# Bucketed attention with a gated convolution layer: value product in two-step groups, rows divided after the product, rounding casts on another engine

## The chip, the cores and the metric

The kernel runs on one core of one Trainium2 chip. A core has engines that work side by side, each through its own list of instructions in order: PE (TensorE, matrix products; its weight loads are shown apart as PEld), DVE (VectorE), ACT (ScalarE), POOL (GpSimd), and SP, which here only issues DMAs. PE writes only to PSUM, a small memory beside it; POOL in this kernel works on SBUF alone. The metric is the device time of one execution in microseconds (us); the figure of a kernel is the median of its timed runs.

## The reference

There are 4 batches of 8 heads, 768 positions and head size 64. A query and a key may meet only if six sign bits of their projections agree.

```python
mask = q_bucket[:, :, :, None] == k_bucket[:, :, None, :]
scores = scale * np.matmul(q, k.transpose(0, 1, 3, 2))
scores = np.where(mask, scores, -1000000000.0)
scores = scores - np.max(scores, axis=-1, keepdims=True)
attn = np.exp(scores)
attn = attn / (np.sum(attn, axis=-1, keepdims=True) + 1e-09)
attn_out = np.matmul(attn, v)                  # then [B, S, H*D] as x
# gate_pre: causal convolution of x over 5 positions, weights conv_w per channel
gate = 1.0 / (1.0 + np.exp(-gate_pre))
out = (gate * (x @ w_val)) @ w_out
```

All is in float32. The second layer (512 by 512 matrices) is computed with three products each, of numbers split into a rounded part and a rest (the kernel calls the rounded type FP32R).

## The kernel before

**Units, tiles, slots.** A unit is one head of one batch (32 units). A tile is 128 queries of a unit against its 768 keys (6 tiles per unit, 192 in all). The main loop (L453) takes one turn, here called a slot, for each tile; everything else is cut into steps that are handed out to the slots. The order of the instructions on PE, ACT, DVE and POOL is the program's own order (`manual_schedule`, L442); SP's order is left to the compiler.

**One slot k** does, in program order: `keep_transposed(k-4)` on ACT (L289, two copies from PSUM to the tiles `pt`); `maxima(k)` (L238), `factors(k)` (L244) and `shifts(k)` (L248) on DVE, which give the bias `nb` and the scale `gs` of the exponential; for every second tile the sums of two tiles plus a small number and their reciprocals on DVE (L262, L266); `normalise(k-2)` on POOL (L271), which divides the 128x768 tile of exponentials `p` in place; `scores(k+1)` on PE (L232, four products into the PSUM tile `s`); `exponentials(k)` on ACT (L256, with the row sum as a by-product); a step of the convolution (every second slot before slot 60), of the loading of weights (L90 to L112, until about slot 50), of the second layer (`moe`, PE L365 and L390), of the operands of a later unit (`prep`, L166 to L176, six DMAs among them), and one step of the value product; last `transposes(k-3)` on PE (L280, six transposes into two PSUM tiles `tp`).

**Buffers that bind.** There are two PSUM tiles `s`, so `scores(k+2)` cannot start before `exponentials(k)` has read its tile, two tiles `tp`, and one PSUM tile `av` for the value product.

**The value product** `attn_v` (L294) is a generator of six steps, one for each block of 128 keys. A step is two products, for the two halves of the queries, placed in the two column halves of the array (`tile_position`); each appears as two instructions, so the profile shows x4 per step. After the sixth step ACT copies the two halves of `av` into rows of `x`, two heads on top of each other (L311). When a pair of heads is there, `pair_x` splits `x` into a rounded part `xh` (DVE, L323) and the rest `xl` (POOL, L324), and computes the convolution on DVE (L332 once, L334 four times); after four pairs ACT applies the sigmoid (L338) and the second layer of that batch begins. There `ht` (L370, DVE) multiplies by the gate, `hh` (L374, DVE) rounds and `hl` (L376, POOL) is the rest.

The second layer gives work to PE in most slots: a step of its first product (L365) or of its second (L390); a batch has 24 and 18 such steps in 48 slots, six of them taken three to a slot, so that about ten slots of each batch have none.

Of the kernel before, what the change touches and what calls it, by code (L numbers as in the profile page):

```python
# [8 lines left out]
FP32 = mybir.dt.float32  # L9
# [12 lines left out]
# the high word of the float64 2**-127, read as a float32; smaller weights count as zero  # L22
# [4 lines left out]
def kernel(  # L27
    ctx: ExitStack,
    tc: tile.TileContext,
    qk: bass.AP,      # [B, H, 128, S]   rows 0-63: q^T, rows 64-127: k^T  # L30
    v: bass.AP,       # [B, H/2, 128, S/128, 128]
    proj: bass.AP,    # [128, 68]  projection, its signs, and what makes the mask's rows of bits
    w_val: bass.AP,   # [128, 4, 512]
    conv_w: bass.AP,  # [128, 20]
    w_out: bass.AP,   # [128, 4, 512]
    out: bass.AP,     # [B, S, 512]
):
    nc = tc.nc
# [7 lines left out]
    LAG = 3  # L46
# [16 lines left out]
    op = ctx.enter_context(tc.tile_pool(name="op", bufs=2))  # L63

# [19 lines left out]
    # Work beside the scores is cut into steps, at most one of a kind in a slot.  # L84

    def from_float64(w, t):
        """Float64 words w, in place: their high words become float32 numbers, their low words what is left."""
# [69 lines left out]
    def prep(i):  # L157
        """The operands of a unit's scores, each [128, S]: two products add up to them."""
# [7 lines left out]
        nc.vector.tensor_copy(out=aq, in_=r)  # L166
# [19 lines left out]
    def bits(i):  # L186
        """The sign bits of four units' queries and keys, each with its complement."""
# [17 lines left out]
    def first_prep():  # L205
        """The first unit's operands, straight from its own queries and keys."""
# [34 lines left out]
    def factors(k):  # L241
        """The scale of a row, or 0 where it has no key in its query's bucket: all its keys count alike then."""
        gs[k] = small.tile([P, 1], FP32, name="gs")
        nc.vector.tensor_scalar(out=gs[k], in0=nms[k], scalar1=BIG / 2, scalar2=scale, op0=ALU.is_lt, op1=ALU.mult)  # L244

    def shifts(k):
        nbs[k] = small.tile([P, 1], FP32, name="nb")
        nc.vector.tensor_tensor(out=nbs[k], in0=nms.pop(k), in1=gs[k], op=ALU.mult)  # L248

    def exponentials(k):  # L250
        s, nb = ss.pop(k), nbs.pop(k)
        p = pp.tile([P, 2, HS], FP32, name="p")
        if k % 2 == 0:
            cur["sm"] = small.tile([P, 2], FP32, name="sm")
        sm = cur["sm"]
        nc.scalar.activation(out=p, in_=s[:, :, 0:HS], func=AF.Exp, bias=nb, scale=gs.pop(k), accum_out=sm[:, k % 2:k % 2 + 1])  # L256
        ps[k] = (p.rearrange("p a b -> p (a b)"), sm)

    # two tiles' sums at a time
    def row_sums(k):  # L260
        sums[k] = small.tile([P, 2], FP32, name="s1")
        nc.vector.tensor_scalar(out=sums[k], in0=ps[k][1], scalar1=1e-9, scalar2=None, op0=ALU.add)  # L262

    def recip(k):
        ri = small.tile([P, 2], FP32, name="ri")
        nc.vector.reciprocal(out=ri, in_=sums.pop(k))  # L266
        rcs[k], rcs[k + 1] = ri[:, 0:1], ri[:, 1:2]

    def normalise(k):
        p, _ = ps[k]  # L270
        nc.gpsimd.tensor_scalar(out=p, in0=p, scalar1=rcs.pop(k), scalar2=1.0, op0=ALU.mult, op1=ALU.mult)  # L271

    def transposes(k):
        p, _ = ps.pop(k)
# [19 lines left out]
    def attn_v(i, pts):  # L294
# [13 lines left out]
        x = cur["x"]  # L308
        for s in range(2):
            o = KW - 1 + s * HS  # L310
            nc.scalar.copy(out=x[hh * D:(hh + 1) * D, o:o + HS], in_=av[s * D:(s + 1) * D, 0:HS])  # L311
# [5 lines left out]
    def pair_x(b, c, x, gs, xs_):  # L317
        for o in (0, HS):
# [4 lines left out]
            nc.vector.tensor_copy(out=xh, in_=x0)  # L323
# [4 lines left out]
        for k in range(KW):  # L328
            yield
            w = cw_sb[:, c * KW + k:c * KW + k + 1]  # L330
            if k == 0:
                nc.vector.tensor_scalar(out=g, in0=x[:, 0:S], scalar1=w, scalar2=None, op0=ALU.mult)  # L332
# [17 lines left out]
    def moe(b, xs_, g):  # L350
# [7 lines left out]
        def val(o, j):  # L358
# [13 lines left out]
            def split():  # L372
                hh = hp.tile([P, HS], FP32R, name="hh")
                nc.vector.tensor_copy(out=hh, in_=ht)  # L374
# [45 lines left out]
    # units of attention: one head of one batch  # L420
# [134 lines left out]
```

## Time and profile before

| what | value |
|---|---|
| time, three runs | median 647.04 us, 646.44 to 647.19 |
| profiled execution | span 645.6 us from the first to the last instruction; the page gives no other time of it |
| instructions | 10637 |
| busy | PE 610.7 us, PEld 412.7, DVE 489.4, ACT 424.5, POOL 355.5 |
| granted TensorE clock | 0.991 on the mean |
| DMA | 56.76 MB, nearly all on SP's queue |

A busy PE is not PE at its peak. Rows of groups show: line, engine, operation, written tile <- read tiles, shape, count, then busy time and mean time of one, then idle time of the engine in front of them. Rows of a timeline show the start, the duration, and the same names. Slots are told apart below by their place in a unit: the product of unit i takes slots 6i+9 to 6i+14.

### The profile page before, as it was taken

The numbers are of one execution on the slowest core, as the hardware profiler recorded it, in microseconds if no ns is written. First come the engines' busy times: TensorE is split into PE (matmuls) and PEld (weight loads), VectorE is DVE, ScalarE is ACT, GpSimd is POOL, SyncE is SP. The second block draws the span as 40 slices with busy tenths as digits, with TensorE's granted clock in tenths as the row PEclk, the third lists the DMA queues.
The fourth block names the chain that finished last, engine by engine and source line by source line (L and its number), as shares of the span: only waits on it lengthen the run. The fifth ranks groups of instructions, "written<-read, shape, count | busy, mean of one in ns | idle before, by whom it ended". The sixth has DMA issues, their size and how long they took to land.

```text
span 645.6 us, 10637 instructions
## 1 busy us (share of the span) xinstructions
PE 610.7 (95%) x3496; PEld 412.7 (64%) x3496; DVE 489.4 (76%) x1064; ACT 424.5 (66%) x881; POOL 355.5 (55%) x326
## 2 busy tenths in 40 slices
PE   4799998988999999999999999999999999999997
PEld 2565554555557666676667776676657777666895
DVE  5788999999996876769785887658695787656532
ACT  3487776767778666667878676576788666665300
POOL 1375868577765663566653656456563566536221
PEclk9799999999999999999999999999999999999999
DMA  6533435343432324233333234243332313300111
GB/s 239 126 100 78 137 102 136 110 123 89 104 78 66 81 66 133 70 103 95 103 79 104 59 79 118 71 117 79 99 75 60 79 30 79 84 18 1 49 50 49
DMA packets 23269, 56.76 MB, mean 88 GB/s; under 512 B 4296, under 2 KB 4296, under 8 KB 23216
## 3 DMA queue, kind: packets, MB, share of 16 engines
q1 hardware_dynamic: 23072, 56.06, 32.2%
q8 instruction: 28, 0.46, 0.3%
q14 instruction: 25, 0.20, 0.1%
q10 hardware_dynamic: 144, 0.03, 0.0%
HBM read 23.12 MB, written 6.29 MB: 46 GB/s over the span
## 4 chain that ended last, share of the span: by engine, by line
PE 70%; DVE 20%; ACT 5%; DMA 2%; issue 2%; POOL 0%; SPq 0%; DVEq 0%; ACTq 0%
PE av L303 17%; PE s L232 16%; PE tp L280 16%; PE m L390 8%; PE m L365 7%; DVE nm L238 7%; DVE nb L248 3%; ACT p L256 2%; DVE g L334 2%; DVE w L100 1%; PE tp L365 1%; PE tp L390 1%; PE s L390 1%; DVE gs L244 1%; PE tp L194 1%
## 5 line engine op out<-in xcount | busy, mean ns | idle before, releaser
L271 POOL TENSOR_SCALAR p<-p,ri 128x768 f32<-128x768 f32 x192 | 211.8, 1108 | 212.6 <-DVE nb L248 142.6
L289 ACT COPY pt<-tp 128x384 f32<-128x384 f32 x384 | 165.2, 481 | 100.9 <-PE tp L280 99.4
L256 ACT ACTIVATE p<-s,nb,gs 128x768 f32<-128x768 f32 x192 | 191.9, 1000 | 56.4 <-DVE nb L248 51.4
L238 DVE TENSOR_REDUCE nm<-s 128x1 f32<-128x768 f32 x192 | 182.5, 951 | 48.3 <-PE s L232 47.7
L280 PEld LDWEIGHTS tp<-ident,p 128*128 128x128 f32 x1152 | 125.4, 142 | 112.5 <-issue 75.4
L280 PE MATMUL tp<-ident,p 128*128 128x128 f32 x1152 | 169.4, 284 | 0.8 <-ACT pt L289 0.4
L303 PE MATMUL av<-pt,vt 128*64 128x384 f32 x768 | 168.7, 511 | 0.3 <-ACT x L311 0.3
L232 PE MATMUL s<-ak,aq 76*128 76x384 f32 x384 | 118.0, 388 | 24.9 <-ACT p L256 20.3
L232 PE MATMUL s<-bk,bq 128*128 128x384 f32 x384 | 102.2, 348 | 0.0
L232 PEld LDWEIGHTS s<-ak,aq 76*128 76x128 f32 x384 | 59.5, 195 | 36.9 <-ACT p L256 29.2
L303 PEld LDWEIGHTS av<-pt,vt 128*64 128x64 f32 x768 | 41.3, 135 | 58.8 <-issue 51.3
L248 DVE TENSOR_TENSOR nb<-nm,gs 128x1 f32<-128x1 f32 x192 | 73.8, 384 | 3.6 <-DVE ri L266 0.2
L334 DVE SCALAR_TENSOR_TENSOR g<-x,cw_sb,g 128x768 f32<-128x768 f32 x64 | 72.9, 1139 | 0.2
L232 PEld LDWEIGHTS s<-bk,bq 128*128 128x128 f32 x384 | 72.0, 194 | 0.4 <-issue 0.4
L168 POOL TENSOR_TENSOR bq<-r,aq 128x768 fp32r<-128x768 f32 x31 | 58.3, 1882 | 0.5 <-DVE aq L166 0.5
L376 POOL TENSOR_TENSOR hl<-ht,hh 128x384 fp32r<-128x384 f32 x32 | 32.8, 1026 | 32.3 <-DVE hh L374 32.3
L324 POOL TENSOR_TENSOR xl<-x,xh 128x384 fp32r<-128x384 f32 x32 | 33.2, 1050 | 29.6 <-DVE xh L323 29.6
L365 PE MATMUL m<-xh,wv 128*128 128x384 f32 x200 | 42.6, 337 | 0.0
L311 ACT COPY x<-av 64x384 f32<-64x384 f32 x64 | 30.3, 473 | 17.9 <-PE av L303 17.0
L370 DVE TENSOR_TENSOR ht<-m,g 128x384 f32<-128x384 f32 x25 | 13.9, 557 | 32.8 <-PE m L365 29.1
L256 ACT ACTIVATION_READ_ACCUMULATOR p<-s,nb,gs 128x1 f32 x192 | 38.6, 201 | 0.0
L390 PE MATMUL m<-wo,hh 128*128 128x512 f32 x144 | 38.2, 395 | 0.0
(84 smaller groups left out, 471.5 us busy)
## 6 DMA issues: line engine op xcount, KB each, us to landing
r<-in_qk_dram SPq DMA_DIRECT2D x32, 384.0 KB
vt<-in_v_dram SPq DMA_DIRECT2D x16, 384.0 KB
out_dram<-o SPq DMA_DIRECT2D x24, 256.0 KB
ak<-aq SPq DMA_DIRECT2D x31, 192.0 KB
bk<-aq SPq DMA_DIRECT2D x31, 192.0 KB
bk<-bq SPq DMA_DIRECT2D x31, 192.0 KB
bq<-aq SPq DMA_DIRECT2D x31, 192.0 KB
w<-in_w_val_dram SPq DMA_DIRECT2D x4, 512.0 KB
```

What stands on the lines that cost most here:

```text
L168: nc.gpsimd.tensor_tensor(out=bq, in0=r, in1=aq.bitcast(FP32), op=ALU.subtract)
L232: nc.tensor.matmul(out=s[:, hf, 0:HS], lhsT=lq[0:n, qs], rhs=rk[0:n, hf * HS:(hf + 1) * HS], start=n == M, stop=n == P)
L238: nc.vector.tensor_reduce(out=nm, in_=s[:, :, 0:HS], axis=AX.XY, op=ALU.max, negate=True)
L248: nc.vector.tensor_tensor(out=nbs[k], in0=nms.pop(k), in1=gs[k], op=ALU.mult)
L256: nc.scalar.activation(out=p, in_=s[:, :, 0:HS], func=AF.Exp, bias=nb, scale=gs.pop(k), accum_out=sm[:, k % 2:k % 2 + 1])
L271: nc.gpsimd.tensor_scalar(out=p, in0=p, scalar1=rcs.pop(k), scalar2=1.0, op0=ALU.mult, op1=ALU.mult)
L280: nc.tensor.transpose(out=tp[:, n * P:(n + 1) * P], in_=p[:, kb * P:(kb + 1) * P], identity=ident)
L289: nc.scalar.copy(out=pt[:, :, qo:qo + P], in_=tp[:, 0:HS].rearrange("p (a b) -> p a b", b=P))
L303: nc.tensor.matmul(out=av[s * D:(s + 1) * D, 0:HS], lhsT=vt[:, kb, hh * D:(hh + 1) * D], rhs=pt[kb // 3][:, kb % 3, :], start=(kb == 0), s ...
L334: nc.vector.scalar_tensor_tensor(out=g, in0=x[:, k:k + S], scalar=w, in1=g, op0=ALU.mult, op1=ALU.add)
L365: nc.tensor.matmul(out=acc[:, 0:HS], lhsT=wv[wi][:, c, j * P:(j + 1) * P], rhs=xs_[(c, o)][xi], start=(m == 0), stop=(m == 11))
L390: nc.tensor.matmul(out=acc, lhsT=hs[(o, j)][hi][:, tb * P:(tb + 1) * P], rhs=wo[wi][:, j, :], start=(m == 0), stop=(m == 11))
```

## The change

- The value product takes two steps in every odd slot (6i+9, 6i+11, 6i+13) and none in the even ones, in place of one step in each.
- The tiles `p` are no longer divided. The sums of all six tiles of a unit are kept in one tile `sm`; in slot 6i+7 DVE adds the small number and takes the reciprocals (128x6), SP writes them to DRAM as rows (pieces of 12 bytes) and reads them back twice, each time spread over 64 partitions, into `rb`.
- After the last step of a value product DVE, not ACT, brings `av` to `x`, and multiplies by `rb` as it does so (two instructions of 64x384, which read `rb` with a stride of three numbers).
- `shifts` becomes a tensor_scalar with a per-row scalar, in place of a product of two tensors.
- The roundings `aq`, `xh`, `hh` and the first of the five products of the convolution move from DVE to POOL.
- Transposes follow two slots behind the scores and not three (`LAG`).

```diff
-    LAG = 3
+    LAG = 2
+    rp = ctx.enter_context(tc.tile_pool(name="rp", bufs=2))
+    dp = ctx.enter_context(tc.tile_pool(name="dp", bufs=2, space=bass.MemoryType.DRAM))
...
-        nc.vector.tensor_copy(out=aq, in_=r)
+        nc.gpsimd.tensor_copy(out=aq, in_=r)
...
     def shifts(k):
-        nc.vector.tensor_tensor(out=nbs[k], in0=nms.pop(k), in1=gs[k], op=ALU.mult)
+        nc.vector.tensor_scalar(out=nbs[k], in0=nms.pop(k), scalar1=gs[k], scalar2=None, op0=ALU.mult)
...
-    def row_sums(k):
-        sums[k] = small.tile([P, 2], FP32, name="s1")
-        nc.vector.tensor_scalar(out=sums[k], in0=ps[k][1], scalar1=1e-9, scalar2=None, op0=ALU.add)
-    def recip(k):
-        ri = small.tile([P, 2], FP32, name="ri")
-        nc.vector.reciprocal(out=ri, in_=sums.pop(k))
-    def normalise(k):
-        nc.gpsimd.tensor_scalar(out=p, in0=p, scalar1=rcs.pop(k), scalar2=1.0, op0=ALU.mult, op1=ALU.mult)
+    def row_sums(i):
+        s1 = small.tile([P, KB], FP32, name="s1", bufs=2)
+        nc.vector.tensor_scalar(out=s1, in0=sms.pop(i), scalar1=1e-9, scalar2=None, op0=ALU.add)
+        ri = small.tile([P, KB], FP32, name="ri", bufs=2)
+        nc.vector.reciprocal(out=ri, in_=s1)
+        rows = dp.tile([2, P, KB // 2], FP32, name="rows")
+        nc.sync.dma_start(out=rows.rearrange("s p t -> p s t"), in_=ri.rearrange("p (s t) -> p s t", s=2))
+        rb = rbs[i] = rp.tile([P, P, KB // 2], FP32, name="rb")
+        for s in range(2):
+            nc.sync.dma_start(out=rb[s * D:(s + 1) * D], in_=rows[s].partition_broadcast(D))
...
         for s in range(2):
             o = KW - 1 + s * HS
-            nc.scalar.copy(out=x[hh * D:(hh + 1) * D, o:o + HS], in_=av[s * D:(s + 1) * D, 0:HS])
+            nc.vector.tensor_tensor(out=x[hh * D:(hh + 1) * D, o:o + HS].rearrange("d (t p) -> d t p", p=P),
+                                    in0=av[s * D:(s + 1) * D, 0:HS].rearrange("d (t p) -> d t p", p=P),
+                                    in1=rb[s * D:(s + 1) * D].rearrange("d p t -> d t p"), op=ALU.mult)
...
-            nc.vector.tensor_copy(out=xh, in_=x0)
+            nc.gpsimd.tensor_copy(out=xh, in_=x0)
...
-                nc.vector.tensor_scalar(out=g, in0=x[:, 0:S], scalar1=w, scalar2=None, op0=ALU.mult)
+                nc.gpsimd.tensor_scalar(out=g, in0=x[:, 0:S], scalar1=w, scalar2=None, op0=ALU.mult)
...
-                nc.vector.tensor_copy(out=hh, in_=ht)
+                nc.gpsimd.tensor_copy(out=hh, in_=ht)
...
+            if 2 <= k < N + 2 and tiles[k - 2][1] == KB - 1:
+                row_sums(tiles[k - 2][0])
...
-            step(avs)
+            if k % 2:
+                step(avs)
+                step(avs)
```

28 lines of the change are left out of this document (9 added, 19 removed).

## The prediction

> **What bounds the kernel now.** I read the stages first (columns: stretch, its us, then busy PE, PEld, DVE, ACT, POOL; slots 9 to 50, 51 to 62, 63 to 188), then single slots in order of time, then the groups.
>
> ```profile
> span 645.6 us, 10637 instructions
> 37.86:158.70 120.84, 107.07 (x620) 62.85 (x619) 114.36 (x237) 87.67 (x190) 83.96 (x75) 1.00 0.41 112
> 158.70:190.08 31.38, 29.88 (x179) 18.02 (x178) 30.37 (x63) 24.41 (x53) 22.31 (x20) 1.00 0.39 97
> 190.08:578.83 388.75, 387.81 (x2283) 265.20 (x2282) 286.13 (x653) 278.11 (x576) 214.39 (x198) 1.00 0.31 81
> ```
>
> There are two kernels here. For slots 9 to 50 (weights are still split) DVE is busy for 114.36 of 120.84 us: it sets the pace, 120.84/7 = 17.26 us per unit. From slot 63 on PE is busy for 387.81 of 388.75 us, at full clock (1.00), and the others have room. So what the change does to DVE counts early, what it does to PE's stream counts late. Here is PE in one slot without second-layer work:
>
> ```profile
> 309.41 0.59 PE L232 MATMUL s<-ak,aq 76*128 76x384 f32 x2
> 309.84 0.52 PE L232 MATMUL s<-bk,bq 128*128 128x384 f32 x2
> 310.30 0.87 PE L303 MATMUL av<-pt,vt 128*64 128x384 f32 x4
> 311.09 0.87 PE L280 MATMUL tp<-ident,p 128*128 128x128 f32 x6
> 311.72 0.59 PE L232 MATMUL s<-ak,aq 76*128 76x384 f32 x2
> ```
>
> Start to start it is 0.43, 0.46, 0.79, 0.63: 2.31 us without a gap, in each slot of this kind.
>
> **Part 1: two steps of the value product in one slot.** Early there are slots without a step; and a row of the tail shows steps that follow each other (the second row has the shortest, middle and longest single run, in ns):
>
> ```profile
> 36.82 0.52 PE L232 MATMUL s<-bk,bq 128*128 128x384 f32 x2
> 37.17 0.82 PE L280 MATMUL tp<-ident,p 128*128 128x128 f32 x6
> ```
>
> ```profile
> 595.55 2.92 PE L303 MATMUL av<-pt,vt 128*64 128x384 f32 x16
> L303 PE MATMUL av<-pt,vt x768: 486/486/538, 39.0 to 599.0; 128*64 128x384 f32 x192
> ```
>
> Scores to transposes without a step take 0.35, with one 0.46 + 0.79; the transposes run 0.87 after a step, 0.82 without: a step alone costs 0.90 + 0.05 = 0.95 us. In the tail sixteen starts lie (2.92 − 0.49)/15 = 0.162 apart, so a second step behind the first costs 0.65. A pair of slots saves 0.30 us, 4.62 becomes 4.32; 93 pairs, 28 us if PE were never kept waiting. The new slots are uneven: 2.96 (odd) and 1.36 (even), or with second-layer work 0.70 and 0.94 more each, from these rows (same operation again after 3.01 and 3.25):
>
> ```profile
> 273.07 0.86 PE L365 MATMUL m<-xh,wv 128*128 128x384 f32 x4
> 273.86 0.87 PE L303 MATMUL av<-pt,vt 128*64 128x384 f32 x4
> ...
> 276.08 0.51 PE L365 MATMUL m<-xh,wv 128*128 128x384 f32 x2
> 243.00 1.09 PE L390 MATMUL m<-wo,hh 128*128 128x512 f32 x4
> 244.03 0.87 PE L303 MATMUL av<-pt,vt 128*64 128x384 f32 x4
> ...
> 246.25 0.63 PE L390 MATMUL m<-wo,hh 128*128 128x512 f32 x2
> ```
>
> **Part 2: what the uneven slots do to the chain of scores.** The other engines in the slot at 309.41, and one place where PE did wait:
>
> ```profile
> 310.40 0.96 DVE L238 TENSOR_REDUCE nm<-s 128x1 f32<-128x768 f32 x1 [0.37 <-PE s L232]
> ...
> 311.62 0.14 DVE L248 TENSOR_TENSOR nb<-nm,gs 128x1 f32<-128x1 f32 x1
> 311.67 0.86 ACT L289 COPY pt<-tp 128x384 f32<-128x384 f32 x2 [0.47 <-PE tp L280]
> ...
> 312.42 1.01 ACT L256 ACTIVATE p<-s,nb,gs 128x768 f32<-128x768 f32 x1
> ...
> 327.96 1.49 DVE L248 TENSOR_TENSOR nb<-nm,gs 128x1 f32<-128x1 f32 x1
> ...
> 329.54 0.99 ACT L256 ACTIVATE p<-s,nb,gs 128x768 f32<-128x768 f32 x1 [0.70 <-DVE nb L248]
> ...
> 330.68 0.30 PEld L232 LDWEIGHTS s<-ak,aq 76*128 76x128 f32 x2 [0.34 <-ACT p L256]
> ```
>
> Scores to maximum 0.99; maximum to the end of nb 1.36; nb to the exponential 0.09; exponential to the scores two tiles on 1.14 (329.54 to 330.68). Transposes to copies 0.58 (311.09 to 311.67), copies to exponential 0.75, since ACT has the copies first. Count from the scores of an odd slot. Transposes start 0.63 before its end, at 2.33; copies 2.91; exponential 3.66; scores two slots on not before 4.80. PE would be there at 4.32: without second-layer work a pair takes 4.80, 0.18 more than the 4.62 of before. With a step of the first product (L365) in each slot the transposes come at 3.03 and the scores may start at 5.50; PE comes at 6.02 − 0.30 = 5.72: no wait. With the second product (L390) likewise, at 6.20.
>
> **Part 3: the multiplication out of PSUM on DVE.** It waits for the last step, and behind it in DVE's order stands the next tile's maximum, which ACT and then PE wait for. The nearest row for its price is a product of a PSUM and an SBUF tile of the same length; the far bound is a 64-partition product of two SBUF tiles of twice the length:
>
> ```profile
> 317.21 0.87 PE L303 MATMUL av<-pt,vt 128*64 128x384 f32 x4
> ...
> 318.15 0.97 ACT L311 COPY x<-av 64x384 f32<-64x384 f32 x2
> L370 DVE TENSOR_TENSOR ht<-m,g 128x384 f32<-128x384 f32 x25 | 13.9, 557 | 32.8 <-PE m L365 29.1 <-PE tp L280 3.4
> ```
>
> ```profile
> 5.79 2.46 DVE L217 TENSOR_TENSOR bq<-r,aq 64x768 fp32r<-64x768 f32 x1
> 8.18 0.66 DVE L219 TENSOR_SCALAR aq<-tp,packed 12x384 fp32r<-12x384 f32 x1
> 8.85 1.39 DVE L219 TENSOR_SCALAR ak<-tp,packed 12x384 fp32r<-12x384 f32 x2
> ```
>
> Between 0.56 and 1.23 (half of 2.46); I take 0.56, the row nearest in operands, and twice that with no overlap, 1.14, as the two L219 rows do not overlap either. The Trainium skill, "VectorE: DVE Perf Modes", section "Two Vector instructions with no wait between them", says that an instruction whose operands start in another group of 32 partitions than those of the one before starts only when all earlier ones have finished. By that rule the two halves and the maximum behind them run one after the other, as in the L219 rows; were they to overlap by 0.1 at the two joints, the sum would be 6 us lower.
>
> ACT's copy starts 0.94 after the last step begins, so the multiplication starts 0.94 + 0.65 = 1.59 after the first of two. From there to the scores two slots on: 1.14 + 1.36 + 0.09 + 1.14 = 3.73. With the first product the value product begins at 0.79 + 0.79 = 1.58, so the scores come at 6.90 in place of 5.72, and the unit takes 2 × 5.72 + 6.90 = 18.34, before 6 × 3.01 = 18.06: 0.28 more. With the second product it begins at 0.79 + 1.03 = 1.82, scores at 7.14: 2 × 6.20 + 7.14 = 19.54 against 19.50. Without either at 0.89, scores at 6.21: 2 × 4.80 + 6.21 = 15.81 against 13.86. PE's 0.9 us per unit from part 1 is thus spent again at the end of each unit.
>
> **Part 4: what DVE loses, and the rest.**
>
> ```profile
> L248 DVE TENSOR_TENSOR nb<-nm,gs 128x1 f32<-128x1 f32 x42 | 20.9, 498 | 0.7
> ```
>
> In the early stretch `nb` takes 0.50 on the mean and up to 1.49 at 327.96; where nothing holds it 0.14. As a tensor_scalar, like `gs` before it, I take 0.15: 14.6 us off DVE's 114.4. Fourteen multiplications put back 7.8: 107.6, 15.4 us per unit, before the moved roundings, the first convolution product and two thirds of the sums and reciprocals are taken off. That is below the 15.81 of the chain, so DVE no longer sets the pace there. But its weight work comes in lumps beside the uneven slots; I take 16.2 per unit, between 15.8 (all hidden) and 17.3 (nothing gained).
>
> POOL drops 192 divisions of a whole tile and gets 111 instructions of at most that size; its other users were not waiting for it where PE is busy, so this is priced at nothing; if a rounding came late, the next unit's operands would. Three DMAs per unit join SP's queue, and SP must stand until the row write has landed; behind it wait operands and output stores. No row of before prices such a write and read-back; it costs nothing as long as both come within the six slots (13.9 us at the shortest) from the reciprocals to their use, and everything beyond that falls on DVE's multiplication. I take nothing. ACT loses its copies out of `av`, 0.97 per unit, beside a busy PE. With transposes two slots behind, a tile's exponentials are still done before the scores of the slot may start, so nothing new waits.
>
> **The sum**, against the span of 645.6. Slots 9 to 50: 7 × (16.2 − 17.26) = −7.4. Slots 51 to 62: 2 × 15.81 − 31.38 = +0.2. Slots 63 to 188, 21 units, of which by the batch's 24 and 18 steps about 11 units' worth have the first product, 5.5 the second, 3.5 neither and one the triple steps: 11 × 0.28 + 5.5 × 0.04 + 3.5 × 1.95 = +10.1; less 1.4, since two of the units that end without such work run into a slot with it, less some 3 of waits that this stretch has today, like the one at 327.96: +5.7. Start: −1 by shorter `nb` chains (an estimate: one held as long as at 327.96). Tail: three pairs, −0.9, and a rounding on POOL in the last chain, +0.3. Together −3.1: a span of 642.5. The three runs have a median 1.4 above the span of the profile, 647.04; the forecast is **644 us**.
>
> **Rivals.** (a) *The lumps eat the early gain*: 17.3 per unit in slots 9 to 50, +7.7, **652**. For it: DVE had no idle time there, and odd slots carry convolution steps. Against: the work itself shrinks. It decides from 16.7 per unit on. (b) *The multiplication is slow* (stride of three numbers, 64 partitions): each 0.1 us more costs 0.2 in each of 30 units, 6 us; at 0.9, midway, +20, **664**. From 0.61 each the change no longer wins. The L217 row speaks for it, but POOL was at work on the same tiles' memory then; L370 against. (c) *DMAs late*: SP stands long enough that operands or `rb` come 1 us after their use; 31 units, **675**. No row of before speaks for it, none excludes it. (d) *The end-of-unit wait costs nothing*, because scores run further ahead than I think: slots 63 to 188 gain 63 × 0.30 = 19 in place of losing 5.7, **619**. Against: the wait at 330.68 shows that they do not. (e) *The steps don't follow each other faster*: then the pairs save little, +5 where PE binds, **649**.
>
> **Chances.** Forecast 0.60 (its own range 635 to 649), a 0.16, b 0.10, c 0.04, d 0.06, e 0.04. The range 630 to 658 leaves out c, most of d and b. A difference of 0.2%, 1.3 us, is about what can be told from none. Faster (below 645.7): three quarters of the forecast and d, 0.51; the same: some 0.09 of the forecast and the near ends of a and e, 0.14; slower: the rest, 0.35.
>
> **What would show it.** Right: `av` rows x8 with 1.51 between starts and the transposes' start; the pairs of slots at 5.7 and 6.2; in slot 6i+13 a wait of DVE for PE `av`, the maximum right behind it, and PE waiting for ACT `p` by about 1.2 us once per unit; `nb` at 0.15; units of about 16 us early. Wrong: multiplications far from 0.56, scores waiting for a DMA, or units of 17 us early.

## The result, and the profile after

The changed kernel takes 668.6 us (median; 664.0 to 672.5) against 646.7 (646.4 to 647.2): a ratio of 1.033, with an interval of 1.028 to 1.038. It is slower by 22 us where 3 us less was forecast, and its times scatter by 8.6 us where those of before scatter by 0.8. The page of its profile (span, busy shares, the clock granted to PE in 40 slices, the chain that ended last, groups with busy time, mean ns of one, and idle time before them):

```profile
span 669.1 us, 10171 instructions
PE 595.1 (89%) x3496; PEld 426.7 (64%) x3496; DVE 445.2 (67%) x889; ACT 392.4 (59%) x817; POOL 243.9 (36%) x245
...
PEclk9999899989899999999889999999999999999999
...
PE 52%; DVE 28%; ACT 9%; issue 6%; POOL 3%; DMA 1%; ACTq 0%; SPq 0%; DVEq 0%; POOLq 0%
...
L234 PE MATMUL s<-ak,aq 76*128 76x384 f32 x384 | 118.4, 390 | 58.7 <-ACT p L259 50.1
...
L313 DVE TENSOR_TENSOR x<-av,rb 64x384 f32<-64x384 f32 x64 | 43.0, 672 | 34.9 <-PE av L305 33.8
...
L250 DVE TENSOR_SCALAR nb<-nm,gs 128x1 f32<-128x1 f32 x192 | 41.2, 214 | 7.2 <-DVE gs L246 0.5
```

PE is busy for 16 us less than before (595.1 against 610.7), although some 10 of the 595.1 us are lost at half clock, as shown below; in the 627.5 us kernel of the experiments, without that loss, it is 582.9, so 27.8 less, and part 1 had 28 for the grouping. But PE now waits 50.1 us for exponentials in front of a tile's scores, and DVE waits 33.8 us for the value product in front of the multiplication L313. The three stretches of the prediction (slots 9 to 50, 51 to 62, 63 to 188; columns as there: busy PE, PEld, DVE, ACT, POOL, then the clock):

```profile
34.60:158.40 123.80, 103.48 (x621) 66.89 (x621) 104.77 (x208) 81.29 (x176) 54.63 (x47) 0.97 0.47 119
158.40:192.23 33.83, 29.91 (x176) 19.48 (x177) 25.11 (x52) 22.05 (x49) 13.28 (x12) 0.95 0.39 96
192.23:603.64 411.41, 380.42 (x2284) 278.07 (x2284) 266.79 (x543) 257.58 (x534) 142.53 (x147) 0.99 0.36 87
```

| part of the span | before, us | after, us | difference | forecast |
|---|---|---|---|---|
| up to slot 9 | 37.86 | 34.60 | -3.3 | -1 |
| slots 9 to 50 | 120.84 | 123.80 | +3.0 | -7.4 |
| slots 51 to 62 | 31.38 | 33.83 | +2.4 | +0.2 |
| slots 63 to 188 | 388.75 | 411.41 | +22.7 | +5.7 |
| tail | 66.77 | 65.46 | -1.3 | -0.6 |

In the long stretch PE was busy for 387.81 of 388.75 us; now it idles for 31. In the first one DVE has less work (114.36 to 104.77), and the stretch is longer all the same. The end of one unit with the first product of the second layer, in order of time (rows of PE, DVE and ACT):

```profile
226.24 0.60 PE L234 MATMUL s<-ak,aq 76*128 76x384 f32 x2
...
227.82 1.51 PE L305 MATMUL av<-pt,vt 128*64 128x384 f32 x8
...
229.38 1.36 DVE L313 TENSOR_TENSOR x<-av,rb 64x384 f32<-64x384 f32 x2
...
229.89 0.60 PE L234 MATMUL s<-ak,aq 76*128 76x384 f32 x2
...
230.77 0.96 DVE L240 TENSOR_REDUCE nm<-s 128x1 f32<-128x768 f32 x1
231.38 0.82 PE L282 MATMUL tp<-ident,p 128*128 128x128 f32 x6
231.76 0.15 DVE L246 TENSOR_SCALAR gs<-nm 128x1 f32<-128x1 f32 x1
231.95 0.21 DVE L250 TENSOR_SCALAR nb<-nm,gs 128x1 f32<-128x1 f32 x1
...
232.26 0.99 ACT L259 ACTIVATE p<-s,nb,gs 128x768 f32<-128x768 f32 x1 [1.55 <-DVE nb L250]
...
233.39 0.45 PE L234 MATMUL s<-ak,aq 76*128 76x384 f32 x1 [1.20 <-ACT p L259]
```

This is the chain of the prediction's part 3, link by link. The multiplication starts 1.56 us after the value product (1.59 foreseen). The scores that PE began at 226.24 are long there (PE is at the value product by 227.82), but their maximum stands behind the multiplication in DVE's order and starts at 230.77, when both halves are done. The exponential at 232.26 waits for that maximum, and the scores at 233.39, two slots on, wait for the exponential to free their place in PSUM. They follow 4.01 us after the multiplication's start (3.73 foreseen, with 1.14 for a multiplication that takes 1.36). PE is idle for 1.20 us. What the prediction did not have is what comes after some of these waits (the same columns as the stretches above; each row is 3.41 us, the first three follow each other, and so do the last two):

```profile
324.69:328.10 3.41, 1.50 (x10) 0.85 (x9) 2.34 (x7) 2.40 (x5) 3.33 (x4) 1.00 0.22 60
328.10:331.51 3.41, 3.41 (x15) 1.83 (x12) 1.05 (x3) 0.84 (x3) 0.73 (x1) 0.50 0.20 58
331.51:334.93 3.42, 3.17 (x21) 2.32 (x22) 2.46 (x4) 3.28 (x8) 2.71 (x3) 1.00 0.32 65
82.36:85.77 3.41, 1.82 (x15) 1.55 (x13) 3.24 (x7) 1.69 (x3) 0.00 (x0) 1.00 0.21 66
85.77:89.18 3.41, 3.10 (x19) 1.89 (x20) 3.31 (x7) 2.79 (x8) 0.00 (x0) 1.00 0.17 58
```

After a wait of 1.91 us at 324.9 (first row), PE's granted clock is 0.50 for exactly 3.41 us, and PE is busy throughout at half the speed. In the fourth row PE was busy for a little more, 1.82 us, and the clock after it stayed at 1.00. There are six stretches at half clock (from 68.7, 140.4, 174.5, 328.1, 345.2 and 468.1 us); they lie a whole number of 3.413 us apart, and each costs 1.7 us of PE. That is the 10 us which the mean clock of 0.985 stands for, and the scatter: the four executions had mean clocks of 0.985, 0.980, 0.993 and 0.991 for spans of 669.1, 670.7, 662.1 and 664.4. Less the share that the clock took, all four lie between 657.3 and 659.1. So the clock makes the scatter; without it the kernel would still be some 12 us slower than before.

### The profile page after: what moved, and what is told of

Same layout as the page of the kernel before. It is cut to its first block, busy times and chain, and to the rows that moved or that the text cites. A ratio compares the mean times of both kernels' runs of the same rounds, so it can differ in the third digit from the quotient of the medians.

```text
span 669.1 us, 10171 instructions
## 1 busy us (share of the span) xinstructions
PE 595.1 (89%) x3496; PEld 426.7 (64%) x3496; DVE 445.2 (67%) x889; ACT 392.4 (59%) x817; POOL 243.9 (36%) x245
## 2 busy tenths in 40 slices
DMA packets 37092, 63.15 MB, mean 94 GB/s; under 512 B 14024, under 2 KB 18120, under 8 KB 37040
## 4 chain that ended last, share of the span: by engine, by line
PE 52%; DVE 28%; ACT 9%; issue 6%; POOL 3%; DMA 1%; ACTq 0%; SPq 0%; DVEq 0%; POOLq 0%
PE av L305 16%; PE s L234 14%; DVE nm L240 9%; PE tp L282 9%; ACT p L259 7%; DVE x L313 6%; PE m L394 6%; PE m L369 5%; DVE g L338 4%; DVE nb L250 2%; DVE gs L246 2%; POOL hl L380 1%; ACT pt L291 1%; POOL hh L378 1%; DVE o L94 1%
## 5 line engine op out<-in xcount | busy, mean ns | idle before, releaser
L282 PEld LDWEIGHTS tp<-ident,p 128*128 128x128 f32 x1152 | 131.3, 142 | 74.9 <-issue 36.6
L234 PE MATMUL s<-ak,aq 76*128 76x384 f32 x384 | 118.4, 390 | 58.7 <-ACT p L259 50.1
L282 PE MATMUL tp<-ident,p 128*128 128x128 f32 x1152 | 165.6, 280 | 5.2 <-ACT pt L291 5.2
L305 PE MATMUL av<-pt,vt 128*64 128x384 f32 x768 | 150.2, 514 | 0.8 <-DVE x L313 0.8
L305 PEld LDWEIGHTS av<-pt,vt 128*64 128x64 f32 x768 | 48.4, 139 | 65.5 <-issue 62.0
L338 DVE SCALAR_TENSOR_TENSOR g<-x,cw_sb,g 128x768 f32<-128x768 f32 x64 | 76.7, 1199 | 4.9 <-POOL g L336 4.7
L168 POOL CAST aq<-r 128x768 fp32r<-128x768 f32 x31 | 31.1, 1005 | 128.7 <-PE s L234 114.9
L313 DVE TENSOR_TENSOR x<-av,rb 64x384 f32<-64x384 f32 x64 | 43.0, 672 | 34.9 <-PE av L305 33.8
L327 POOL CAST xh<-x 128x384 fp32r<-128x384 f32 x32 | 16.2, 507 | 116.4 <-DVE x L313 116.4
L378 POOL CAST hh<-ht 128x384 fp32r<-128x384 f32 x32 | 16.2, 506 | 97.1 <-DVE ht L374 87.4
L250 DVE TENSOR_SCALAR nb<-nm,gs 128x1 f32<-128x1 f32 x192 | 41.2, 214 | 7.2 <-DVE gs L246 0.5
```

Source lines behind the costliest of these rows:

```text
L234: nc.tensor.matmul(out=s[:, hf, 0:HS], lhsT=lq[0:n, qs], rhs=rk[0:n, hf * HS:(hf + 1) * HS], start=n == M, stop=n == P)
L250: nc.vector.tensor_scalar(out=nbs[k], in0=nms.pop(k), scalar1=gs[k], scalar2=None, op0=ALU.mult)
L282: nc.tensor.transpose(out=tp[:, n * P:(n + 1) * P], in_=p[:, kb * P:(kb + 1) * P], identity=ident)
L305: nc.tensor.matmul(out=av[s * D:(s + 1) * D, 0:HS], lhsT=vt[:, kb, hh * D:(hh + 1) * D], rhs=pt[kb // 3][:, kb % 3, :], start=(kb == 0), s ...
L313: nc.vector.tensor_tensor(out=x[hh * D:(hh + 1) * D, o:o + HS].rearrange("d (t p) -> d t p", p=P), in0=av[s * D:(s + 1) * D, 0:HS].rearran ...
L338: nc.vector.scalar_tensor_tensor(out=g, in0=x[:, k:k + S], scalar=w, in1=g, op0=ALU.mult, op1=ALU.add)
```

## The experiments

Theory A: the loss is made at the end of a unit, where the multiplication holds up the next maximum; PE waits, and its clock drops after some of the waits. Theory B: the work moved to POOL comes late. Theory C: the uneven slots lose by themselves.

| kernel | us | ratio to before, interval |
|---|---|---|
| changed kernel | 668.6 | 1.033, 1.028 to 1.038 |
| multiplication behind the next maximum | 627.5 | 0.970, 0.968 to 0.971 |
| one step of the value product per slot | 649.4 | 1.004, 1.002 to 1.005 |
| before, steps grouped | 641.3 | 0.991, 0.989 to 0.993 |
| before, shift as tensor_scalar | 642.6 | 0.993, 0.992 to 0.995 |
| before, both | 638.1 | 0.986, 0.984 to 0.988 |
| before, both, and ACT's copies later | 647.2 | 1.000, 0.999 to 1.001 |
| changed, eight idle products at a unit's end | 677.3 | 1.047, 1.044 to 1.049 |
| changed, four | 667.8 | 1.031, 1.029 to 1.032 |
| changed, four where there is a wait | 663.7 | 1.026, 1.024 to 1.028 |
| changed, reciprocals read without a stride (wrong factors) | 662.0 | 1.022, 1.019 to 1.026 |
| the 627.5 us kernel, roundings and product on DVE | 633.0 | 0.977, 0.976 to 0.979 |
| the 627.5 us kernel, first product alone on DVE | 627.4 | 0.970, 0.968 to 0.971 |
| the 627.5 us kernel, first product with a second operation | 627.5 | 0.970, 0.968 to 0.972 |
| the 627.5 us kernel, exponential ahead of the copies | 663.8 | 1.025, 1.024 to 1.027 |
| the 627.5 us kernel, exponential ahead, four buffers | 648.1 | 1.002, 1.000 to 1.003 |
| the 627.5 us kernel, rows written in reading order | 671.3 | 1.036, 1.033 to 1.040 |

### The multiplication behind the next maximum

```diff
-        for s in range(2):
-            ... multiply av by rb into x
+        def multiply():
+            for s in range(2):
+                ... multiply av by rb into x
+        outs.append(multiply)
...
                 shifts(k)
+            while outs:
+                outs.pop(0)()
```

> The changed kernel, but DVE gets the two multiplications of a unit behind the maximum, the factor and the shift of the next tile instead of ahead of them. Nothing else moves; the whole result is computed. Theory A (the end of a unit: the multiplication holds up the next maximum, PE then waits 1.2 to 2.4 us, and in the changed kernel's profile six of these waits were followed by a stretch of 3.41 us at half the granted clock, 10 us in all): the waits of PE for the exponentials at a unit's end go, and the half-clock stretches with them; units with the first product at 17.2 us (three pairs of 5.72), without second-layer work at 14.4 to 14.6; span 622 to 640, below the kernel before. Theory B (the roundings and the first convolution product on POOL come late): those are where they were, so 655 or more. Theory C (the uneven slots themselves lose): still 655 or more.

627.5 us: 41 us less than the changed kernel and 19.5 less than the kernel before, by the order of two instructions on one engine. Its stretches, and the end of the same unit:

```profile
34.44:149.60 115.16, 100.54 (x620) 65.74 (x620) 106.53 (x207) 81.02 (x176) 55.43 (x47) 1.00 0.50 127
149.60:179.27 29.67, 28.13 (x176) 18.71 (x177) 24.49 (x52) 21.98 (x49) 14.23 (x12) 1.00 0.43 112
179.27:560.00 380.73, 373.02 (x2288) 274.99 (x2286) 268.79 (x542) 257.05 (x534) 140.04 (x144) 1.00 0.39 94
```

```profile
214.14 1.51 PE L305 MATMUL av<-pt,vt 128*64 128x384 f32 x8
...
215.50 0.95 DVE L240 TENSOR_REDUCE nm<-s 128x1 f32<-128x768 f32 x1
...
216.21 0.60 PE L234 MATMUL s<-ak,aq 76*128 76x384 f32 x2
...
216.80 1.35 DVE L315 TENSOR_TENSOR x<-av,rb 64x384 f32<-64x384 f32 x2
216.98 0.99 ACT L259 ACTIVATE p<-s,nb,gs 128x768 f32<-128x768 f32 x1
...
218.27 0.60 PE L234 MATMUL s<-ak,aq 76*128 76x384 f32 x2
```

The maximum starts while the value product still runs, the multiplication comes after the shift, and the scores follow each other after 2.06 us without a wait. From the first scores of one unit to those of the next it takes 17.14 us where the first product runs all through (17.2 expected; 18.6 in the changed kernel, 18.04 before). No half-clock stretch is left, the clock is 1.00 in all three rows. Theory A holds; B and C fall as causes of the loss, since the work on POOL and the uneven slots are all still there.

### One step per slot, grouping alone, shift alone, both

```diff
-            if k % 2:
-                step(avs)
-                step(avs)
+            step(avs)
```

> The changed kernel with one step of the value product in every slot, as before the change; the multiplication stays where the change put it, ahead of the next maximum. Theory A: the wait at a unit's end becomes shorter by the 0.65 us of the second step but stays; the saving of 0.30 us per pair is lost; units without second-layer work at about 15.0 instead of 16.1, with the first product about 18.5; few half-clock stretches, since the waits stay near 1 us; 650 to 660. Theory B: no change, 665 to 670. Theory C: back to 647 or below.

649.4: just below the 650 to 660 of A, and 2.4 above the 647 of C, so the time alone is a narrow judge between them. The units are as A had them: those without second-layer work are shorter by a part of the wait (15.08 against 16.14), those with the first product stay as they were (18.55 against 18.60), since the shorter wait gives back about what the longer pairs take, and no stretch is at half clock. C is out by the first experiment and by the next one: with slots just as uneven, both kernels are faster than the kernel before.

The next two are the kernel before with `step(avs)` twice in odd slots, and with `nb` as a tensor_scalar:

> The kernel before with one edit: two steps of the value product in each odd slot, none in an even one. The copy out of the value product's PSUM stays on ACT, behind that slot's exponential. Theory A: pairs with second-layer work at 5.72 and 6.20, pairs without at 4.80; the copy on ACT costs some 0.5 us per unit in place of the 1.2 to 2.4 of the multiplication on DVE; 638 to 648. Theory C: the uneven slots carry most of the loss, 655 or more. Theory B says nothing of this one beyond no loss.

> The kernel before with one edit: the shift nb by a tensor_scalar with the factor as its scalar. The prediction priced this at 14.6 us less of DVE's time in slots 9 to 50, where DVE set the pace. If that price holds and DVE sets the pace there: 637 to 643, the first stretch 5 to 8 us shorter, later stretches unchanged. If the first stretch is bound by the chain of scores, maxima and exponentials rather than by DVE's total: 645 to 648, no change.

641.3 and 642.6: both gain. Grouping takes 5.0 us off the long stretch (383.72) and none off the first (121.21); the shift takes 3.0 off the first stretch (117.83) and 1.5 off the long one. 14.6 us of DVE's time had been set down for the shift there; DVE's busy time in that stretch fell by 5.3 (114.36 to 109.05), though `nb` itself went from 20.9 to 8.9. In the kernel before, the 19 rows of `nb` over 0.25 us in that stretch end 11 to 21 ns after a row of POOL ends. With the new shift other rows of DVE are long in their place. The first product of a convolution, 0.61 us on DVE in the kernel before, is one:

```profile
80.48 1.83 POOL L168 TENSOR_TENSOR bq<-r,aq 128x768 fp32r<-128x768 f32 x1
...
80.83 0.21 DVE L248 TENSOR_SCALAR nb<-nm,gs 128x1 f32<-128x1 f32 x1
...
80.96 1.77 DVE L332 TENSOR_SCALAR g<-x,cw_sb 128x768 f32<-128x768 f32 x1
```

It ends 0.42 us after POOL's row, and so do all three of its kind in the stretch. So the long rows of `nb` were time spent beside POOL, and of the 12 us taken off `nb` more than half came back in other rows.

> The kernel before with two edits, the shift as a tensor_scalar and two steps of the value product in odd slots; ACT's copies out of the value product's PSUM stay ahead of the next exponential. Alone the grouping gave 641.3 us and the shift 642.6; the two with the copies moved behind the exponential gave 647.2. If the gains of the two add up: 636 to 638, and the move of the copies cost the difference. If the two edits get in each other's way (both shorten the same stretch): 640 to 643 and the moved copies cost 4 to 7. If it is again near 647: the copies' place is not it.

638.1: the gains of the two add up (5.6 + 4.4 = 10, measured 9). With ACT's copies out of `av` moved behind the next exponential as well, the mirror image of the first experiment, it was otherwise:

> The kernel before (division on POOL ahead of the transposes, roundings on DVE, no way through DRAM) with three edits: the shift as a tensor_scalar, two steps of the value product in odd slots, and ACT's two copies out of the value product's PSUM behind the exponential of the next slot instead of ahead of it. If the division by rows of reciprocals and the move of the roundings carry part of the gain of the 627.5 us kernel: 632 or more. If grouping, shift and a free end of the unit are all of it: 626 to 631, with units at 17.1 (first product) and 14.6 (none).

647.2, 9 us more than with the copies left in place, so this run cannot tell what it was made for. From slot 69 on every second unit became longer, by 0.4 to 1.8 us, in its first odd slot (4.76 instead of 3.67 in the one shown):

```profile
354.35 0.97 ACT L313 COPY x<-av 64x384 f32<-64x384 f32 x2
354.57 0.59 PE L232 MATMUL s<-ak,aq 76*128 76x384 f32 x2
...
354.85 1.68 DVE L326 CAST xh<-x 128x384 fp32r<-128x384 f32 x2 [2.42 <-ACT x L313]
...
356.72 0.94 DVE L238 TENSOR_REDUCE nm<-s 128x1 f32<-128x768 f32 x1
...
359.33 0.62 PE L232 MATMUL s<-ak,aq 76*128 76x384 f32 x2 [0.86 <-ACT p L256]
```

DVE's rounding `xh`, which is due once per pair of heads and so in every second unit, now waits for the late copies, and the next maximum stands behind it: 35.4 us of such waits in all, 9.3 in the 638.1 us kernel. It is the loss of theory A again, through another instruction. Later is not always better: it depends on who needs the result. The parts are told by the pair of 638.1 and 627.5 instead: what the change has beyond grouping and shift (the multiplication out of PSUM, the way through DRAM, the roundings on POOL, transposes one slot earlier) is worth 10.6 us once it is in the right order.

### The clock

```diff
+            if k % 6 == 2 and k > 13:
+                for n in range(8):
+                    nc.tensor.matmul(out=cur["av"][:, HS:512], lhsT=ident, rhs=ident, start=True, stop=True)
```

> The changed kernel, with eight idle products of the identity with itself (128 x 128, into unused columns of the value product's PSUM tile) put in PE's order where it waits at a unit's end, ahead of the scores after slot 6i+14. They change no result and take nothing away: the multiplication still holds up the maximum, only PE is busy for some 1.2 to 1.7 us of the wait. Theory A (a wait that leaves PE busy for less than about half of a stretch of 3.41 us is followed by such a stretch at half clock): the half-clock stretches go, the waits stay as end-of-unit time; 656 to 664, against 668.6. If the clock is not lowered by PE's idle time: half-clock stretches as before, 668 to 680.

677.3: by its time in the range of the rival (668 to 680) and not in A's. But the half-clock stretches, which the rival wanted as before, are gone except one after the start. One idle product takes 0.275 us, so eight are longer than most of the waits, and their price hides what the clock gave back. Then four:

> The changed kernel with four idle products at a unit's end instead of eight. Eight took 2.2 us, more than most of the waits (1.2 to 1.9 us), and cost 0.3 us per unit and 2 us where there was no wait. Four take 1.1 us. Theory A (PE's idle share of a stretch of 3.41 us sets the next one's clock): no or one half-clock stretch after the start, the waits kept: 656 to 663, against 668.6. If the clock falls for another reason: 666 to 676, with four to eight such stretches.

667.8: again a time in the rival's range (666 to 676), with the stretches as A had them, one after the start (at 339.9) in place of six. By units the two are told apart: five units that had held a half-clock stretch are 1.55 to 1.70 us shorter, and four units in which second-layer work filled the gap pay 0.9 to 1.0 us for products that they didn't need. So the same four without those places:

> The changed kernel with the four idle products only where the changed kernel's trace has a wait at a unit's end: not at the five units where a batch's second-layer work fills the gap, nor in the tail. In the run with four everywhere each of four such places cost 0.9 to 1.1 us, the tail 1.1, and these hid what the clock gave back (units 2, 6, 8, 16 and 23 of the comparison were 1.55 to 1.70 us shorter). The clock loss of the changed kernel's four runs, span times (1 - clock), is 10.0, 13.4, 4.6 and 6.0 us, 8.5 on the mean. Theory A: most of this comes back and nothing is paid: 660 to 665, at a mean clock of 0.993 or more. If the clock is lowered by something else: 667 to 672.

663.7, as A had it. Its stretches:

```profile
34.43:155.05 120.62, 106.75 (x676) 72.31 (x676) 104.74 (x208) 81.19 (x176) 54.61 (x47) 1.00 0.49 121
155.05:187.35 32.30, 30.18 (x192) 20.60 (x192) 25.10 (x52) 22.03 (x49) 13.27 (x12) 1.00 0.41 103
187.35:595.72 408.37, 390.72 (x2404) 290.60 (x2404) 266.83 (x543) 257.22 (x534) 142.36 (x147) 1.00 0.36 88
```

PE has more to do than in the changed kernel and is done sooner: 3.2, 1.5 and 3.0 us by stretch, 7.7 between the two profiled executions (4.9 between the medians; the changed kernel's profiled execution is one of its slower ones). Units without a half-clock stretch are unchanged (18.60 and 18.62), so the wait itself is still there, and five of the six half-clock stretches are gone. It is PE's idle time that lowers its clock.

### The price of the multiplication

```diff
-                                    in1=rb[s * D:(s + 1) * D].rearrange("d p t -> d t p"), op=ALU.mult)
+                                    in1=rb[s * D:(s + 1) * D].rearrange("d p t -> d (p t)").rearrange("d (t p) -> d t p", p=P), op=ALU.mult)
```

> The changed kernel, with the reciprocals read by the multiplication in the order in which they lie instead of with a stride of three numbers. So the rows get the wrong factors; the work is the same. It tells whether the stride makes the multiplication 0.67 us instead of the 0.56 foreseen, and what a tenth of a microsecond costs there. If it is the stride: multiplication at 0.55 to 0.58, 0.2 us less in each of 30 units, and fewer half-clock stretches: 655 to 664. If it is the 64 partitions or PSUM: 0.67 again, 662 to 673.

662.0, and the row of the multiplication (shortest, middle and longest in ns):

```profile
L313 DVE TENSOR_TENSOR x<-av,rb x64: 539/555/562, 46.6 to 610.6; 64x384 f32<-64x384 f32 x64
```

The 0.56 of the prediction was right for an operand that lies in order; the stride of three numbers costs 0.117 us more per instruction, and 6.6 us in all by the medians: 5.6 us per tenth, where rival (b) had 6. The times of the two kernels scatter by 5.5 and 8.6 us, so the units are the better measure: one with the first product all through takes 18.38 where it took 18.61, the 0.23 of two instructions. To write the rows so that they can be read in order, with the right factors, in the 627.5 us kernel:

```diff
-        rows = dp.tile([2, P, KB // 2], FP32, name="rows")
+        rows = dp.tile([2, KB // 2, P], FP32, name="rows")
...
-        rb = rbs[i] = rp.tile([P, P, KB // 2], FP32, name="rb")
+        rb = rbs[i] = rp.tile([P, KB // 2, P], FP32, name="rb")
```

> The kernel with the multiplication behind the next maximum (627.5 us), with the reciprocals written to DRAM tile by tile, so that the multiplication reads them without a stride of three numbers: 0.555 us each instead of 0.672, with the right factors. Nothing waits for the multiplication there any more, so late it gains nothing; early DVE is busy most of the time and gets 0.23 us per unit back: 624 to 627. If the write in pieces of 4 bytes comes late: PE or DVE waiting for a DMA, 628 or more.

671.3: the multiplication takes 0.555 and waits for its rows (groups by tile: what DVE waited for in front of it, in us and times):

```profile
L315 DVE TENSOR_TENSOR x<-av,rb x64: 537/555/564, 46.8 to 626.9; 64x384 f32<-64x384 f32 x64
...
  DMA rb<-rows: 18.4, 9
```

The three times as many pieces (53476 packets in all against 37092) hold SP: from the reciprocals to the issue of the second read it takes 14.9 us in the middle of 32 units, against 4.4 in the changed kernel, where between the issue of that read and the multiplication 4.6 us are left at the least. The other operands wait behind in the same queue (PE waits 9.2 us for `bq`, in three places), and the mean clock of PE is 0.969. So rival (c) can happen; the change stood clear of it.

### What lies on POOL

> The kernel with the multiplication behind the next maximum (627.5 us), with the three kinds of roundings (of the queries and keys, of the attention's result, of the gated values) and the first convolution product back on DVE. The prediction priced their move to POOL at nothing late, and as a gain for DVE early. If that holds: slots 9 to 50 longer by 2 to 6 us, as DVE gets 7 roundings of 0.5 to 0.6 us and some products back, the rest the same within 1; 629 to 634. If POOL's slowness costs (a 2.2 us product ahead of four DVE ones, roundings late): faster than 627.5, 622 to 627.

633.0: the move is worth 5.5 us, 2.0 of them before slot 9, 2.4 in the long stretch.

> The kernel with the multiplication behind the next maximum (627.5 us), with the first convolution product alone back on DVE (0.61 us there, 2.2 us on POOL) and the roundings left on POOL. If POOL's long product delays the chain of a convolution (DVE waits for it 4.7 us in all, and its next products run beside it): 625 to 627. If it lies beside other work, as the prediction had it: 627 to 630, as DVE gets 16 products back early and late.

627.4, no difference. The product on POOL has room.

```diff
-                nc.gpsimd.tensor_scalar(out=g, in0=x[:, 0:S], scalar1=w, scalar2=None, op0=ALU.mult)
+                nc.gpsimd.tensor_scalar(out=g, in0=x[:, 0:S], scalar1=w, scalar2=1.0, op0=ALU.mult, op1=ALU.mult)
```

> The kernel with the multiplication behind the next maximum (627.5 us), with the first convolution product on POOL written with a second operation, a multiplication by 1.0, as the division of the kernel before had it. That division took 0.91 to 1.13 us on POOL for a tile of the same size, the product without a second operation 2.21 us. If the form makes the price: 0.9 to 1.1 us here, and 626 to 628 for the kernel, as nothing waits much for this product. If the operands do (four more columns per row, another pool): 2.2 us again, 627 to 628.

627.5; the row of the product here, and after it that of the changed kernel:

```profile
L339 POOL TENSOR_SCALAR g<-x,cw_sb x16: 902/906/1077, 72.5 to 582.1; 128x768 f32<-128x768 f32 x16
```

```profile
L336 POOL TENSOR_SCALAR g<-x,cw_sb x16: 2206/2212/2395, 75.7 to 625.8; 128x768 f32<-128x768 f32 x16
```

So it is the form that makes the price of this product on POOL, and the kernel's time does not change with it.

### ACT's exponential ahead of the copies

```diff
-            if 0 <= k - LAG - 1:
+            if k % 2 and 0 <= k - LAG - 1:
                 keep_transposed(k - LAG - 1)
...
                 exponentials(k)
+            if k % 2 == 0 and 0 <= k - LAG - 1:
+                keep_transposed(k - LAG - 1)
```

> The kernel with the multiplication behind the next maximum (627.5 us), with one more exchange: in even slots ACT gets the exponential ahead of the two copies of the transposed tile. The prediction's chain for a pair of slots without second-layer work is transposes, copies, exponential, scores: 4.80 us against PE's 4.32. If this chain sets that pace: pairs without second-layer work at 4.3 to 4.6, such units at 13.3 to 14.0 in place of 14.6, the units with second-layer work unchanged at 17.1 and 18.5; 621 to 626. If not: 627 to 630.

663.8: the experiment did not do what it was for. The exponential's row names why:

```profile
442.49 0.99 ACT L259 ACTIVATE p<-s,nb,gs 128x768 f32<-128x768 f32 x1 [2.24 <-PE tp L282]
```

It waits for transposes: with three buffers, tile k takes the place of tile k-3, which is transposed at the end of the slot before.

> The trial with ACT's exponential ahead of the copies in even slots again, with four buffers for the exponentials instead of three (and one instead of two for the broadcast reciprocals, to make room). With three, the exponential of tile k had to wait for the transposes of tile k-3, so the exchange could not work: 663.8 us. With four the exponential is free of them. If the chain transposes, copies, exponential, scores sets the pace of pairs without second-layer work, as the prediction had it: such units at 13.3 to 14.2 in place of 14.6, others at 17.1 and 18.5; 621 to 627. If something else holds them: 627 to 631.

648.1. To make room, the broadcast reciprocals have one buffer in place of two here; no multiplication waits for its rows in this trace. In a unit without second-layer work the exchange does what it was for:

```profile
304.67 0.59 PE L234 MATMUL s<-ak,aq 76*128 76x384 f32 x2
...
307.61 0.60 PE L234 MATMUL s<-ak,aq 76*128 76x384 f32 x2
...
309.35 0.60 PE L234 MATMUL s<-ak,aq 76*128 76x384 f32 x2
```

The pairs take 4.68 to 4.77 us and the unit 14.13, within the 13.3 to 14.2 expected, against 4.80 to 4.84 and 14.46 in the 627.5 us kernel: the chain did set the pace of such pairs, if by little. Elsewhere the copies now come late: PE waits 33.8 us for ACT's copies in front of the transposes (1.1 in the 627.5 us kernel), and there are six half-clock stretches (mean clock 0.984). So the exchange as a whole gives nothing.

## Why the prediction was wrong

**Part 1, right.** Eight products take 1.51 us; pairs with the first product take 3.65 + 2.06 = 5.71 (5.72 forecast).

**Part 2, right.** A pair without second-layer work in the changed kernel (PE's rows in order of time):

```profile
315.55 0.58 PE L234 MATMUL s<-ak,aq 76*128 76x384 f32 x2 [0.29 <-issue]
...
318.49 0.59 PE L234 MATMUL s<-ak,aq 76*128 76x384 f32 x2
...
320.34 0.61 PE L234 MATMUL s<-ak,aq 76*128 76x384 f32 x2 [0.24 <-ACT p L259]
```

2.94 + 1.85 = 4.79, against 4.80. That neither part loses by itself is shown by the kernel before with grouping alone (641.3).

**Part 3, the mechanism right, a size and a consequence missing.** Place, chain and unit times came as worked out; the term that was mis-sized is the multiplication, 0.67 and 0.67 instead of 0.56 and 0.56, because its price was taken from a row whose operands lie in order. (The 1.14 of the sum is 0.02 more than twice 0.56.) That the two halves and the maximum do not overlap was right: the halves take 1.36 together, and the maximum starts 1.39 after the first. With 0.23 us more per unit the forecast units become 18.57 with the first product (measured 18.60), 16.04 without second-layer work (16.14), and 19.53 with the second product in five slots and the first in one (19.55). The step that failed is "PE's 0.9 us per unit from part 1 is thus spent again": a wait was priced at its length. Six times PE was idle for so much of a stretch that it ran the next at half clock. The four idle products where there is a wait gave back 7.7 us of this between the profiled executions; one such stretch stayed.

**Part 4, wrong in its premise.** The forecast set DVE's pace (15.4 to 16.2 per unit) and the chain at the unit's end (15.81) side by side and took little more than the larger, so that early the wait cost nothing. They add in part: with the clock undisturbed the first stretch takes 120.62 with the wait and 115.16 without it, 0.78 us per unit, about half of what the wait costs a unit without second-layer work (16.14 against 14.46). Without it the stretch is 16.45 per unit, close to the 16.2 taken. The 14.6 us that the shift was to take off DVE's time were 5.3 in the run with the shift alone, since the long rows of `nb` were time beside POOL. The new shift took 0.214 us and not 0.15, 2.7 us more in that stretch; what that cost is not shown. That the roundings on POOL cost nothing was right, and more: the move gained 5.5 us. That the DMAs cost nothing was right: no multiplication waited for its rows.

**The sum.** The forecast was a span of 642.5, the profile has 669.1, 26.6 more. Half-clock stretches make 7.7 shown and about 1.7 for the one that stayed; the early waits 5.5; the stride in the long stretch 4.8 (408.37 with four idle products at the waits, 403.57 with the reciprocals read without a stride, each with one half-clock stretch there); the deductions of 1.4 and 3 us for the long stretch did not show up in it, 4.4 (argued from the sum; no run takes them apart); the early rate 1.8; start and tail gained 3.0 more than forecast. That is 22.9. Some 4 us, in units where second-layer work starts or stops, have no cause assigned. Without its half-clock stretches the kernel would still be some 15 us above the forecast span and above that of the kernel before: the other terms alone turn the forecast's gain into a loss.

**The rivals.** (a) came true in its number, a first stretch that gains nothing, but not by its reason: with the multiplication behind the maximum the same weight work goes with 115.16 us. (b) came true in part, 0.67 on the way to 0.9, at the slope foreseen. (c) did not happen. (d) is what the 627.5 us kernel is, by another order: its long stretch gains 8.0, not the 19 of the rival. (e) fell. None of them had the clock.

## What to carry to other kernels

An instruction that waits is priced by what is queued behind it: before giving an engine on the path of the scores a new job at the end of a product, put it behind the work that others wait for, and see who needs its result (after DVE's multiplication nothing urgent did; after ACT's copies a rounding on DVE did, with the next maximum behind it). A wait of PE of some 1.7 us or more can cost 1.7 us beyond itself, so look at the granted clock in the stretch after the wait. A long row next to another engine's work is not time that goes away with that instruction. Take an instruction's price from a row with the same strides and the same operations, not only the same size.

## What the runs showed of the hardware

**PE's clock falls after waits far shorter than 3.4 us.** Worked out from the rows of PE: of the 3.41 us stretches on the grid in which the half-clock ones lie, the six in which PE was busy for a share of 0.51 or less were followed by one at half clock, the next (0.54, the stretch at 82.36 above) was not. The kernels with reciprocals read without a stride, with four buffers and with four idle products have the same line: half clock after 0.43 to 0.52, full clock from 0.52 or 0.53 on. In the kernel before with grouping alone it fits less well: half after 0.66 once, full after 0.56. In the kernel with rows written in reading order, a stretch with 0.46 was followed by full clock once, and PE idled through that one. So the line is near one half, and not sharp. The Trainium skill, "TensorE: Matmul & The Clock Gate", section "What's actually happening", gives a free-running window of 3413 ns, and the trace agrees (stretches of 3.413 us, on one grid). The same section of the Trainium skill lets the clock fall after an idle window of about 3.4 us; here waits of 1.66 to 2.41 us were enough, and the measurement decides.

**POOL's tensor_scalar with one operation takes 2.21 us, with a second (times 1.0) 0.91**, for the same 128x768 float32 tile.

**Rows of DVE end with rows of POOL.** In the first stretch of the kernel before, `nb` takes 0.14 to 0.21 us in 23 of 42 rows; the 19 longer ones (up to 1.49) each end 11 to 21 ns after a row of POOL. With another form of the shift it takes 0.21 in the same place, and other rows of DVE are long beside POOL.

**A stride of three numbers in one SBUF operand** takes DVE's product of 64x384 with a PSUM operand from 0.555 to 0.672 us.
